# Four modulation vectors gathered as one in the set of step 16, the rows' scales on GpSimd, and a copy of sums moved behind the logarithms

## The chip, the cores and the metric

The kernel runs on one core of one Trainium2 chip. A core has five engines that work side by side, each on its own queue in order: PE (TensorE, matrix products), ACT (ScalarE, activation functions and copies), DVE (VectorE, element by element), POOL (GpSimd, element by element, without access to PSUM) and SP (SyncE, which here only starts DMA transfers). They wait for one another on semaphores. SBUF holds operands, PSUM holds the sums that PE writes. The metric is the time of one execution on the device in microseconds (us), the median of several runs; lower is better.

## What is computed

The reference, cut to what matters here:

```python
mod = (silu(c) @ w_mod).reshape(6, 448)          # six vectors of 448
sa, ca, ga, sb, cb, gb = mod                     # mod[0] ... mod[5] in the kernel
h = layernorm(x) * (1 + ca) + sa                 # x: 2048 tokens x 448 channels
x = x + ga * S4D(h)                              # a long convolution per channel, by FFT in the reference
h = layernorm(x) * (1 + cb) + sb
x = x + gb * mixer(h)                            # token-mixing MLP, 2048 -> 1792 -> 2048
```

`S4D` builds for each of 448 channels a kernel of 2048 taps out of 256 complex exponentials, and convolves. The kernel does the convolution with its own two-stage transform. Since the transform is linear, `ga` is multiplied into the vectors before it: mod[1] becomes (1 + ca) * ga and mod[0] becomes sa * ga.

## The kernel before

The first half of the program makes the convolution kernels, in 56 steps of 8 channels' worth each (`NHALF = 56`). A step `s` needs, of PE, a phase (`st_phase`) and exponents (`st_exponents`), of ACT magnitudes (`st_exp`) and sines (`st_step`), of DVE four products that fill the tile E, of POOL two products that fill the tile G and one (`st_mag2`, tile m), and of PE, two steps later, the sum over both (`st_kgen`, tile kg in PSUM, one buffer). Every second sum is copied by ACT out of PSUM into the tile ks, and POOL adds the skip term every fourth time. E has three buffers in the pool `gp_`, taken in turn.

Exponential and sine are in different function tables of ACT, and loading a table takes time. So the magnitudes of eight steps are made together: `window(s)` at s = 0, 8, 16, 24 and 32 runs the set of eight. It begins with `angle()` and `logs()`, an arctangent and logarithms of the next channels' parameters, then takes `e` from 0 to 7: two magnitudes on ACT (`st_exp`), the next exponents on PE, whatever copies wait in the lists `dve` and `act` (`flush`), some steps of the parameters' chain (`more`, DVE and POOL), and one piece of other work. After the set the steps s to s + 7 follow.

Other work in the sets of steps 8 and 16:

- **Rows** (`u_rows`, 32 of them, L588 on PE and L592 on DVE): the first transform of the layer-normed input. A row takes a table `wur` made on POOL (`u_table`, L571) from the inverse deviation `rs`, and DVE multiplies PE's output by mod[1] and stores it to DRAM (`yu_d`). `rs` is worked out in `logs(True)` by an exponential of a logarithm, and improved by a Newton step in `u_scale`, six small operations on DVE (L552 to L558). `u_means` transforms the means.
- **Columns** (`u_cols`, L624 on PE, L628 on DVE), from step 17 on: the second transform, which reads the rows back and adds mod[0].
- **Modulation** (`modulation(k, half)`): half 0 multiplies the four row blocks of `w_mod` for vector k, each with 32 columns of the activated c, into four blocks of 32 partitions of one PSUM tile (L534, 8 matmul instructions, as each product in this type is two passes), and ACT copies it to SBUF (`parts`, L536). Half 1 adds the four blocks up and spreads them to all partitions by a product with the matrix `sums`, whose rows 0, 32, 64 and 96 are one and the others zero (L530, 2 instructions), and ACT copies this to `mod[k]` (L531). Vectors 1 and 2 are made in steps 4 to 7, vector 0 in the set of step 8, vectors 4, 5 and 3 in the set of step 16.

All these PE outputs (rows, columns, modulation, `st_s1`) take turns in the pool `pms` of three PSUM tiles.

The order on PE, ACT, DVE and POOL is written out by hand (`tc.manual_schedule`): instructions run in the order in which the program emits them. SP is so up to step 8 (`first.close()`); behind it a planner places the DMA starts by its own estimates. `late` gives loads by step: of `w_mod`, vector 2 in step 4, vector 0 in step 7 into a part of the tile `wm0`, vectors 4, 5 and 3 in steps 12 to 14 into parts of `xt` whose rows are done. PE's fillers `warm(n)` (L676) write into the unused half of kg's tile.

At step 7, the sums of step 5 wait to be copied by ACT (L775) and are flushed at the end of the step, in front of the set of step 8:

```python
            if s == NHALF - 1:
                break
            flush(act)
```

and in the set of step 16 the modulation stands at these places:

```python
                for k, e0 in ((4, 1), (5, 3), (3, 6)) if s == 16 else ():
                    if e in (e0, e0 + 1):
                        modulation(k, e - e0)
```

Behind the 56 steps come the rest of the convolution and the token-mixing MLP, which is a long run of matmuls with the weights streamed in.

Of the kernel before, what the change touches and what calls it, by code (L numbers as in the profile page):

```python
# [22 lines left out]
P = 128  # L23
# [209 lines left out]
def tile_adaln_s4d_mixer(ctx, tc, i, out):  # L233
# [19 lines left out]
    with ExitStack() as es:  # L253
# [96 lines left out]
        def wm_slot(k):  # L350
# [8 lines left out]
                wm_load(0, wm_slot(0)),  # L359
# [10 lines left out]
            14: lambda: wm_load(3, xt[0:PP, 8:12, 0:D]),  # L370
        }
# [122 lines left out]
        def logs(root=False):  # L494

            for a, s, u, xa, ya in tmp.values():
                S.activation(u, ya, AF.Square)
                S.activation(s, s, AF.Ln)
                S.activation(u, u, AF.Ln, bias=1.0)
            if root:  # L500
                S.activation(rs, mv[:, :, 1], AF.Ln, bias=eps_t)
                S.activation(rs, rs, AF.Exp, scale=-0.5)
            for q, (a, s, u, xa, ya) in tmp.items():
                S.activation(a, a, AF.Exp, bias=ldt[:, q : q + 1])
            tmp.clear()
# [32 lines left out]

        mv = xp.tile([P, 16, 2], F32, name="mv")
        rs = xp.tile([P, 16], F32, name="rs")  # L540
        nm = xp.tile([P, 16], F32, name="nm")
# [7 lines left out]

        def u_scale():  # L550

            tt(nm, rs, rs, ALU.mult)  # L552
            stt(nm, mv[:, :, 1], EPS, nm, ALU.add, ALU.mult)
            ts(nm, nm, -0.5, 1.5, ALU.mult, ALU.add)
            tt(rs, rs, nm, ALU.mult)
            for h in range(2):
                p = slice(64 * h, 64 * h + 64)
                stt(means[p, h], mv[p, :, 0], -1.0, rs[p], ALU.mult, ALU.mult)  # L558
# [187 lines left out]
        fresh, ready, hold, soon, due = [], [], [], [], []  # L746
# [342 lines left out]
        def window(s):  # L1089
# [3 lines left out]
            logs(s == 8)  # L1093
            if s == 8:
                more(10)
                u_scale()
                u_table(0)
                u_table(1)

            if s == 0:  # L1100
                st_exponents(s)
            for e in range(BATCH):
# [9 lines left out]
                if s == 8 and e == 0:  # L1112
                    tt(mod[1], mod[1], mod[2], ALU.mult)
# [4 lines left out]
                if s == 8 and e in (3, 4):  # L1118
                    modulation(0, e - 3)
                if s == 8 and e == 5:  # L1120

                    G.tensor_tensor(mod[0], mod[0], mod[2], ALU.mult)
# [7 lines left out]
                for k, e0 in ((4, 1), (5, 3), (3, 6)) if s == 16 else ():  # L1130
                    if e in (e0, e0 + 1):
                        modulation(k, e - e0)
# [5 lines left out]
                if s in (8, 16):  # L1138
                    some(u_rows, rows, ((0, 2, 2, 2, 2, 0, 2, 2) if s == 8 else (2, 2, 2, 2, 2, 0, 1, 1))[e])
# [23 lines left out]
        for s in range(NHALF):  # L1163
# [55 lines left out]
            if s == NHALF - 1:  # L1219
                break  # L1220
            flush(act)
# [372 lines left out]
```

## Time and profile before

| what | us |
| --- | --- |
| median of 3 runs (lowest, highest) | 666.34 (666.05, 667.45) |
| the profiled execution, its own time | 666.04 |
| its span in the trace | 664.3 |
| PE busy | 612.2 (92%) |
| DVE busy | 444.1 (67%) |
| ACT busy | 440.9 (66%) |
| POOL busy | 269.5 (41%) |

The span is the time from the first to the last recorded instruction; the rest of the time lies around it. Busy shares over the whole span say little here, since the first half (the steps, up to about 330 us) and the second (the MLP) have different limits: POOL works in the first half only. The views are read by stage: the chain of waits follows the work that ended last back from the end, the timeline lists an engine's instructions (start, length, engine, line, operation, output and inputs, shapes, count, and in brackets the idle time in front and who ended it), and the stretches give each engine's busy time between two times. Lines such as L588 are those of the printed code.

### The profile page before, as it was taken

The page shows a single profiled execution, that of the slowest core. Times are in us where ns is not written, and L with a number is a line of the kernel's source. Part 1 is how long each engine was busy: PE and PEld are TensorE (multiplying, and loading weights), DVE is VectorE, ACT ScalarE, POOL GpSimd, SP SyncE. Part 2 cuts the span into 40 slices and gives each one's busy share as a digit, 9 for nine tenths or more (in the row PEclk, how much of TensorE's full clock was granted, in tenths as well). Part 3 has the DMA queues.
Part 4 walks back from the last instruction along what each step waited for, and adds up shares of the span by engine and source line. Part 5 has one row for each costly group of instructions (what it writes and reads, how often), then busy time and mean ns, then how long its engine had stood idle before and what let it go on. Part 6 is the DMA issues. An engine that isn't in the chain of part 4 may idle for free.

```text
span 664.3 us, 19155 instructions
## 1 busy us (share of the span) xinstructions
PE 612.2 (92%) x7639; PEld 442.8 (67%) x7639; DVE 444.1 (67%) x852; ACT 440.9 (66%) x828; POOL 269.5 (41%) x350
## 2 busy tenths in 40 slices
PE   1868998999999999999898999999999999999997
PEld 0544455445455555656554667788999999999997
DVE  8999889798893877868665677787522553333331
ACT  6978898999889999999587578886222532222220
POOL 7885597498599788797562000000000000000000
PEclk9999999999999999999999989999999999999999
DMA  6695747598876457676787999946665165555530
GB/s 159 195 222 171 271 136 245 213 269 238 230 263 190 66 160 204 186 210 193 236 279 218 257 241 232 218 117 195 181 179 149 59 197 165 162 160 163 166 113 28
DMA packets 98833, 125.14 MB, mean 188 GB/s; under 512 B 13780, under 2 KB 80120, under 8 KB 98744
## 3 DMA queue, kind: packets, MB, share of 16 engines
q1 hardware_dynamic: 97928, 121.30, 64.6%
q0 software_dynamic: 816, 2.62, 1.6%
q8 instruction: 60, 0.98, 0.7%
q14 instruction: 29, 0.24, 0.1%
HBM read 88.53 MB, written 34.87 MB: 186 GB/s over the span
## 4 chain that ended last, share of the span: by engine, by line
PE 58%; ACT 11%; DMA 10%; DVE 7%; POOL 6%; issue 4%; SPq 2%; DVEq 0%; ACTq 0%; POOLq 0%
PE o L1560 7%; PE o L1562 7%; PE o L1561 7%; PE acc L1397 6%; PE acc L1398 6%; PE acc L1399 6%; PE xe L664 5%; PE kg L761 4%; DMA us_d<-uo 3%; PE xg L664 2%; POOL G L734 2%; DMA w<-in_B_w_dram 2%; POOL G L735 2%; PE vv L892 2%; ACT mag L693 2%
## 5 line engine op out<-in xcount | busy, mean ns | idle before, releaser
L218 ACT CAST whi<-w 128x896 fp32r<-128x896 f32 x64 | 59.7, 939 | 138.6 <-PE o L1561 81.5
L227 DVE TENSOR_TENSOR wlo<-w,whi 128x896 fp32r<-128x896 f32 x64 | 68.1, 1086 | 41.8 <-ACT whi L218 38.7
L734 POOL TENSOR_TENSOR G<-mag,gs 128x512 f32<-128x512 f32 x56 | 71.9, 1284 | 37.4 <-ACT gs L730 37.4
L1397 PE MATMUL acc<-h3h,whi 128*128 128x448 f32 x224 | 83.7, 374 | 3.0 <-ACT h3h L1470 1.4
L1398 PE MATMUL acc<-h3l,whi 128*128 128x448 f32 x224 | 81.9, 365 | 0.4 <-DVE mean L1418 0.2
L1399 PE MATMUL acc<-h3h,wlo 128*128 128x448 f32 x224 | 81.6, 364 | 0.0
L1560 PE MATMUL o<-uh,whi 128*128 128x448 f32 x224 | 81.3, 363 | 0.0
L1562 PE MATMUL o<-uh,wlo 128*128 128x448 f32 x224 | 81.2, 362 | 0.0
L1561 PE MATMUL o<-ul,whi 128*128 128x448 f32 x224 | 80.6, 360 | 0.0
L761 PEld LDWEIGHTS kg<-E,G 128*32 128x32 f32 x3584 | 54.2, 111 | 32.9 <-issue 20.9
L735 POOL TENSOR_TENSOR G<-mag,gs 128x512 f32<-128x512 f32 x56 | 72.0, 1287 | 0.0
L761 PE MATMUL kg<-E,G 128*32 128x64 f32 x3584 | 63.5, 222 | 7.5 <-issue 5.4
L664 PE MATMUL xg<-tab,lph 64*128 64x512 f32 x112 | 62.2, 555 | 7.0 <-DVE E L740 3.0
L1565 DVE TENSOR_TENSOR y<-o,x 128x448 f32<-128x448 f32 x16 | 10.0, 625 | 78.8 <-PE o L1562 78.8
L664 PE MATMUL xe<-tab,lph 64*128 64x512 f32 x112 | 62.2, 555 | 0.4 <-issue 0.4
L714 POOL TENSOR_TENSOR m<-mag,w 128x512 f32<-128x512 f32 x53 | 55.8, 1052 | 4.2
L1397 PEld LDWEIGHTS acc<-h3h,whi 128*128 128x128 f32 x224 | 42.5, 190 | 16.2 <-ACT h L1469 3.5
L1398 PEld LDWEIGHTS acc<-h3l,whi 128*128 128x128 f32 x224 | 42.4, 189 | 3.4 <-DVE h3l L1467 0.5
L1399 PEld LDWEIGHTS acc<-h3h,wlo 128*128 128x128 f32 x224 | 42.4, 189 | 3.3
L1562 PEld LDWEIGHTS o<-uh,wlo 128*128 128x128 f32 x224 | 42.1, 188 | 3.4
L1561 PEld LDWEIGHTS o<-ul,whi 128*128 128x128 f32 x224 | 41.9, 187 | 3.0
L1560 PEld LDWEIGHTS o<-uh,whi 128*128 128x128 f32 x224 | 42.0, 188 | 2.1
(256 smaller groups left out, 1391.5 us busy)
## 6 DMA issues: line engine op xcount, KB each, us to landing
w<-in_B_w_dram SPq DMA_DIRECT2D x64, 224.0 KB
w<-in_B_w_dram SPq DMA_DIRECT2D x32, 448.0 KB
yi<-yu_d SPq DMA_DIRECT2D x32, 224.0 KB
us_d<-uo SPq DMA_DIRECT2D x16, 448.0 KB
u<-us_d SPq DMA_DIRECT2D x64, 112.0 KB
v_d<-vt SPq DMA_DIRECT2D x32, 224.0 KB
vt<-v_d SPq DMA_DIRECT2D x14, 448.0 KB
yu_d<-yt SPq DMA_DIRECT2D x13, 448.0 KB
```

Source lines behind the costliest of these rows:

```text
L218: self.nc.scalar.copy(hi, w)
L227: eng.tensor_tensor(lo, w, hi.bitcast(F32), ALU.subtract)
L664: T.matmul(out[k], lhs[r], rhs[r], start=start, stop=stop)
L734: G.tensor_tensor(Gt[:, 1], mg_, v32(sg), ALU.mult)
L735: G.tensor_tensor(Gt[:, 0], mg_, v32(cg_), ALU.mult)
L761: T.matmul(kg[32 * q : 32 * q + 32, m], Gt[:, c, d], E[:, c, d], start=h == 0 and c == 0 and m == 0, stop=h == 1 and c == 1, skip_group_ch ...
L1397: nc.tensor.matmul(acc[f], hi[:, fs], h3h[:, r], start=r == 0, stop=False)
L1398: nc.tensor.matmul(acc[f], hi[:, fs], h3l[:, r], start=False, stop=False)
L1399: nc.tensor.matmul(acc[f], lo[:, fs], h3h[:, r], start=False, stop=r == 15)
L1560: nc.tensor.matmul(o, hi[:, ks], uh[kh][:, k], start=kh == 0 and k == 0, stop=False)
L1561: nc.tensor.matmul(o, hi[:, ks], ul[kh][:, k], start=False, stop=False)
L1562: nc.tensor.matmul(o, lo[:, ks], uh[kh][:, k], start=False, stop=kh == 1 and k == 6)
```

## The change

It has four parts.

1. The four vectors 0, 4, 5 and 3 are made together in the set of step 16. `gathered` adds the four row blocks of each vector up within PSUM, vector n in partitions 32n to 32n + 31 of one tile, in two calls (e = 2, 3) with 16 matmul products in all and one copy to SBUF. `spread` takes the 32 rows of each vector with the same 32 rows of `sums` to all partitions, two vectors per call (e = 4, 6), each with its copy to `mod[k]`. Vector 0's modulation leaves the set of step 8, and its product with mod[2] on POOL moves to e = 6 of the set of step 16. The load of its weights leaves step 7 and goes, in step 16, into a tile of E's ring.
2. The operations of `u_scale` go from DVE to POOL, with two new preparations (`u_ready`: variance plus epsilon, and the negative mean) at the end of step 7. They and the first two row tables are now emitted ahead of ten steps of the parameters' chain. The product mod[1] * mod[2] goes from DVE to POOL.
3. ACT's copy of the sums of step 5 goes from the end of step 7 to between the logarithms and the exponentials in the set of step 8.
4. The rows of the set of step 16 are placed differently: 2, 2, 2, 0, 1, 1, 2, 2 instead of 2, 2, 2, 2, 2, 0, 1, 1 by e, as far as rows are left.

```diff
@@ -356,7 +356,6 @@
         late = {
             4: lambda: wm_load(2, wm_slot(2)),
             7: lambda: [
-                wm_load(0, wm_slot(0)),
                 nc.sync.dma_start(svt, i["SV"]),
                 s2_load(0),
                 s2_load(1),
@@ -368,6 +367,11 @@
             12: lambda: wm_load(4, xt[0:PP, 0:4, 0:D]),
             13: lambda: wm_load(5, xt[0:PP, 4:8, 0:D]),
             14: lambda: wm_load(3, xt[0:PP, 8:12, 0:D]),
+            16: lambda: wm_load(
+                0,
+                gp_.tile([P, 2, GD, NJ], F32, tag="E", name="wE").rearrange("p a g j -> p (a g j)")[0:PP, 0 : 4 * D]
+                .rearrange("p (q d) -> p q d", q=4),
+            ),
         }
 
 
@@ -491,7 +495,7 @@
 
             if q > 1:
                 yield from angles()
-        def logs(root=False):
+        def logs(root=False, inside=()):
 
             for a, s, u, xa, ya in tmp.values():
                 S.activation(u, ya, AF.Square)
@@ -499,6 +503,9 @@
                 S.activation(u, u, AF.Ln, bias=1.0)
             if root:
                 S.activation(rs, mv[:, :, 1], AF.Ln, bias=eps_t)
+            for f in inside:
+                f()
+            if root:
                 S.activation(rs, rs, AF.Exp, scale=-0.5)
             for q, (a, s, u, xa, ya) in tmp.items():
                 S.activation(a, a, AF.Exp, bias=ldt[:, q : q + 1])
@@ -536,9 +543,32 @@
             act.append(lambda: S.copy(pmods[k], pm))
 
 
+        group = (0, 4, 5, 3)
+
+        def gathered(q0):
+
+            if q0 == 0:
+                pmods["all"] = pms.tile([P, D], F32, tag="ms", name="pm")
+            pm = pmods["all"]
+            for q in range(q0, q0 + 2):
+                for n, k in enumerate(group):
+                    T.matmul(pm[32 * n : 32 * n + 32], scb[:, q], wms[k][:, q], start=q == 0, stop=q == 3)
+            if q0:
+                pmods["all"] = qp.tile([P, D], F32, tag="parts", name="parts")
+                act.append(lambda: S.copy(pmods["all"], pm))
+
+        def spread(n0):
+
+            for n in range(n0, n0 + 2):
+                k, r = group[n], slice(32 * n, 32 * n + 32)
+                pm = pms.tile([P, D], F32, tag="ms", name="pm")
+                T.matmul(pm, sums[r], pmods["all"][r], start=True, stop=True)
+                act.append(partial(S.activation, mod[k], pm, AF.Copy, bias=1.0 if k in (1, 4) else 0.0))
+
+
         mv = xp.tile([P, 16, 2], F32, name="mv")
         rs = xp.tile([P, 16], F32, name="rs")
-        nm = xp.tile([P, 16], F32, name="nm")
+        nm, ve, minus = (xp.tile([P, 16], F32, name=k) for k in ("nm", "ve", "minus"))
         means = xp.tile([P, 2, 16], F32, name="means")
         G.memset(means, 0.0)
 
@@ -547,15 +577,20 @@
             V.bn_stats(st, xt[:, r])
             V.bn_aggr(mv[:, r], st)
 
+        def u_ready():
+
+            G.tensor_scalar(ve, mv[:, :, 1], EPS, None, ALU.add)
+            G.tensor_scalar(minus, mv[:, :, 0], -1.0, None, ALU.mult)
+
         def u_scale():
 
-            tt(nm, rs, rs, ALU.mult)
-            stt(nm, mv[:, :, 1], EPS, nm, ALU.add, ALU.mult)
-            ts(nm, nm, -0.5, 1.5, ALU.mult, ALU.add)
-            tt(rs, rs, nm, ALU.mult)
+            G.tensor_tensor(nm, rs, rs, ALU.mult)
+            G.tensor_tensor(nm, ve, nm, ALU.mult)
+            G.tensor_scalar(nm, nm, -0.5, 1.5, ALU.mult, ALU.add)
+            G.tensor_tensor(rs, rs, nm, ALU.mult)
             for h in range(2):
                 p = slice(64 * h, 64 * h + 64)
-                stt(means[p, h], mv[p, :, 0], -1.0, rs[p], ALU.mult, ALU.mult)
+                G.tensor_tensor(means[p, h], minus[p], rs[p], ALU.mult)
 
         def u_means():
 
@@ -743,7 +778,7 @@
 
         kgs, kss, made_k = {}, {}, [0]
 
-        fresh, ready, hold, soon, due = [], [], [], [], []
+        fresh, ready, hold, soon, due, kept = [], [], [], [], [], []
 
         def mellow():
             ready.extend(fresh)
@@ -1090,12 +1125,13 @@
             if s:
                 aside.append(True)
             angle()
-            logs(s == 8)
+            logs(s == 8, kept)
+            kept.clear()
             if s == 8:
-                more(10)
                 u_scale()
                 u_table(0)
                 u_table(1)
+                more(10)
 
             if s == 0:
                 st_exponents(s)
@@ -1110,16 +1146,11 @@
                 flush(dve)
                 flush(act)
                 if s == 8 and e == 0:
-                    tt(mod[1], mod[1], mod[2], ALU.mult)
+                    G.tensor_tensor(mod[1], mod[1], mod[2], ALU.mult)
                 if s < 32:
                     more(WPACE[s // 8][e])
                 if s == 0 and e >= 4:
                     u_stats(e - 4)
-                if s == 8 and e in (3, 4):
-                    modulation(0, e - 3)
-                if s == 8 and e == 5:
-
-                    G.tensor_tensor(mod[0], mod[0], mod[2], ALU.mult)
                 if s and e < (2 if s <= 32 else 1):
                     st_kgen(s - (2 if s <= 32 else 1) + e)
                 elif e == 5 and s < 24:
@@ -1127,16 +1158,20 @@
                         yks[0] = y0.tile([P, 32, DC], F32, tag="yk", name="yk0")
                     st_s1(act)
 
-                for k, e0 in ((4, 1), (5, 3), (3, 6)) if s == 16 else ():
-                    if e in (e0, e0 + 1):
-                        modulation(k, e - e0)
+                if s == 16 and e in (2, 3):
+                    some(u_rows, rows, (2, 0)[e - 2])
+                    gathered(2 * e - 4)
+                elif s == 16 and e in (4, 6):
+                    spread(e - 4)
+                if s == 16 and e == 6:
+                    G.tensor_tensor(mod[0], mod[0], mod[2], ALU.mult)
 
                 if s == 8 and e == 0:
                     warm(7)
                 if s == 8 and e == 1:
                     u_means()
                 if s in (8, 16):
-                    some(u_rows, rows, ((0, 2, 2, 2, 2, 0, 2, 2) if s == 8 else (2, 2, 2, 2, 2, 0, 1, 1))[e])
+                    some(u_rows, rows, ((0, 2, 2, 2, 2, 0, 2, 2) if s == 8 else (2, 2, 0, 0, 1, 1, 2, 2))[e])
                 elif s == 24 and e in (0, 2, 4, 6, 7):
                     some(u_cols, cols, 1)
 
@@ -1218,6 +1253,9 @@
                     piece(False, True)
             if s == NHALF - 1:
                 break
+            if s == 7:
+                kept.append(act.pop())
+                u_ready()
             flush(act)
 
             if s in (1, 2):
```

## The prediction

> **What bounds the kernel now.** I read the page's first lines, then the chain of waits, then the busy time by stretches around the two stages that the diff touches, then the timelines of single engines there.
>
> ```profile
> span 664.3 us, 19155 instructions
> ```
>
> The profiled execution took 666.04 us, 1.74 more than its span. The median of the three runs is 666.34, so a shift of the span by x is forecast as 666.34 + x. The edits lie in the eight-step sets at steps 8 and 16: there all steps' exponents are computed by TensorE and turned into magnitudes on ScalarE, and row and modulation work lies between. First the chain around the set of step 8 (start, length, what):
>
> ```profile
> 66.12 0.99 DVE mod L1113
> ...
> 68.67 1.82 PE pu L588 x4
> ...
> 70.72 0.89 PE pm L534 x8
> 71.61 0.95 PE pu L588 x3
> ...
> 72.95 0.95 PE pm L530 x2
> 73.90 0.96 PE pu L588 x3
> ...
> 82.75 1.28 POOL G L734
> ```
>
> TensorE carries this stage, and both halves of a modulation vector, L534 and L530, are links of it. At 82.75 GpSimd takes over: its work per step sets the pace of the steps behind, so an earlier 82.75 moves all of steps 8 to 15. Now the set of step 16 (per stretch: length, then busy time and count of PE, PEld, DVE, ACT, POOL, then clock, DMA):
>
> ```profile
> 115.00:120.00 5.00, 5.00 (x148) 2.96 (x139) 3.20 (x6) 4.62 (x10) 3.57 (x6) 1.00 0.23 79
> 120.00:125.00 5.00, 4.73 (x22) 1.42 (x18) 4.66 (x11) 4.07 (x8) 3.37 (x8) 1.00 0.84 314
> 125.00:130.00 5.00, 4.84 (x87) 2.46 (x87) 2.81 (x7) 4.88 (x13) 1.59 (x3) 1.00 0.62 228
> ```
>
> PE is busy 14.57 of 15 us, ACT 13.57. Work added to PE there has no cover, and ACT is nearly full itself. The set ends where ACT reaches the first step's work, and GpSimd starts from there:
>
> ```profile
> 133.06 1.27 POOL L734 TENSOR_TENSOR G<-mag,gs 128x512 f32<-128x512 f32 x1 [4.13 <-ACT gs L730]
> ...
> 135.52 0.24 POOL L709 TENSOR_TENSOR w<-mag 128x16 f32<-128x16 f32 x1
> 135.84 1.05 POOL L714 TENSOR_TENSOR m<-mag,w 128x512 f32<-128x512 f32 x1
> 136.84 1.28 POOL L734 TENSOR_TENSOR G<-mag,gs 128x512 f32<-128x512 f32 x1
> ```
>
> GpSimd idles 4.13 us for ACT, then runs back to back, 3.78 us per step. Whatever the set of step 16 loses ahead of 133.06, the rest keeps.
>
> **Part 1: the front of the set of step 8.** ACT and GpSimd as they are:
>
> ```profile
> 59.15 0.37 ACT L775 COPY ks<-kg 128x256 f32<-128x256 f32 x1 [0.83 <-PE kg L676]
> ...
> 63.69 0.21 ACT L502 ACTIVATE rs<-rs 128x16 f32<-128x16 f32 x1
> 65.45 1.18 POOL L571 TENSOR_TENSOR wur<-wu,rs 128x256 f32<-128x256 f32 x2
> 68.73 1.28 DVE L592 SCALAR_TENSOR_TENSOR yt<-pu,means,mod 128x448 f32<-128x448 f32 x2
> ```
>
> The copy of the sums keeps ACT idle 0.83 us for TensorE's filler matmuls. Behind the logarithms it finds them done: the logarithms and the square root's exponential come about 0.84 us earlier (63.69 to 62.85), and so do the first magnitudes and TensorE's next exponents. The copy then ends near 61.6; queued behind it are the exponentials (counted), and on PE the next kernel sums, which need its PSUM tile:
>
> ```profile
> 61.68 1.10 PE L761 MATMUL kg<-E,G 128*32 128x64 f32 x64
> ```
>
> They start at 61.68, so this wait costs nothing to 0.2; I take nothing. Against it, the rows' scales go to GpSimd, ahead of two tables, a split (cast and difference) and now the product that every row's output on DVE needs (formerly DVE's 0.99 at 66.12):
>
> ```profile
> L709 POOL TENSOR_TENSOR w<-mag 128x16 f32<-128x16 f32 x56 | 14.2, 254 | 2.2 <-ACT mag L693 1.3 <-DVE yk L805 0.8
> L401 POOL CAST hl<-xa 128x256 fp32r<-128x256 f32 x2 | 0.8, 398 | 5.8 <-DVE xa L442 5.8
> L403 POOL TENSOR_TENSOR hl<-xa,hl 128x256 fp32r<-128x256 f32 x2 | 1.5, 740 | 0.2
> L1122 POOL TENSOR_TENSOR mod<-mod,mod 128x448 f32<-128x448 f32 x1 | 1.1, 1139 | 1.1 <-ACT mod L531 1.1
> ```
>
> From 63.06: four dependent small operations at 0.32 (135.52 to 135.84 above), two at 0.2, tables 1.18, split 0.40 + 0.74, product 1.14: 63.06 + 1.28 + 0.4 + 1.18 + 1.14 + 1.14 = 68.2, with gaps 68.35. The first row output starts then, not at 68.73: **0.35 gained**. No row shows GpSimd's scalar form, used by one of the six and, in step 7, by the two preparations; I price it as L709, between nothing and the cast's 0.40. The preparations run where GpSimd waits for ACT. Bounds of this part: 0.85 if the product isn't awaited, -0.2 if GpSimd is slower.
>
> [...]
>
> **Part 2: the modulation vector taken out of the set of step 8.** Gone from PE are L534 (0.89 on the chain) and L530 (0.95), with two copies on ACT and a product on GpSimd. Next late would be the ring of three PSUM tiles between PE (1.34 for a pair of rows and its exponents, 71.61 to 72.95) and DVE's outputs (1.28 a pair). The two alternate, so I let 0.2 of the 1.84 come back: **1.65 gained**, bounds 1.2 and 1.84. DVE has 2.0 us less time in this set, and is rid of the product's 0.99 and of six small scale operations; I take it to fit, and a lateness up to 1.2 would be hidden in its wait at step 10:
>
> ```profile
> 89.37 0.69 DVE L736 TENSOR_TENSOR E<-m,xe 128x512 f32<-128x512 f32 x1 [1.24 <-POOL w L709]
> ```
>
> Parts 1 and 2: 82.75 comes **2.0 earlier**, bounds 1.0 and 2.7. The vector's load leaves the queue in step 7, where no step waits for it.
>
> **Part 3: the set of step 16.** PE and ACT now:
>
> ```profile
> 118.28 0.94 PE L534 MATMUL pm<-xt,scb 112*32 112x448 f32 x8
> 119.15 1.02 PE L588 MATMUL pu<-xt,wur 64*128 64x448 f32 x4
> ...
> 120.33 1.02 PE L530 MATMUL pm<-parts,sums 128*128 128x448 f32 x2
> 121.28 0.64 PE L588 MATMUL pu<-xt,wur 64*128 64x448 f32 x1
> 121.29 0.49 PE L664 MATMUL xe<-tab,lex 64*128 64x512 f32 x1
> 121.76 0.54 PE L588 MATMUL pu<-xt,wur 64*128 64x448 f32 x1
> ```
> ```profile
> 123.54 0.53 ACT L536 COPY parts<-pm 128x448 f32<-128x448 f32 x1
> 123.97 0.60 ACT L693 ACTIVATE mag<-xe 128x512 f32<-128x512 f32 x1
> ...
> 126.72 1.07 ACT L805 COPY yk<-y 128x512 f32<-128x512 f32 x2
> 127.68 0.61 ACT L693 ACTIVATE mag<-xe 128x512 f32<-128x512 f32 x1
> ...
> 128.65 0.56 ACT L536 COPY parts<-pm 128x448 f32<-128x448 f32 x1
> 129.06 0.35 ACT L448 ACTIVATE xa<-A_C_real 128x128 f32<-128x128 f32 x1
> ...
> 129.47 0.63 ACT L726 ACTIVATE ab<-xe 128x512 f32<-128x512 f32 x1
> ```
>
> Eight L534 (four row blocks, two passes, column groups side by side) take 0.94. The gather needs 32, so 2 x 1.9, where three vectors took 3 x 0.94. A spread of two vectors takes 1.02 if its quarters run side by side, as the halves do (four L588 in 1.02, where one row's two passes alone take 121.28 to 122.30). Ahead of the first step's phase, PE then has 3.8 + 2.04 against 2.82 + 2.04 (the third old sum came behind it): about 1.0 more.
>
> In the clock of before: the first old gather is gone at 118.28, so a pair of rows starts there; with the exponents between them it takes 1.2 (119.15 to 120.33), the last row 1.0 to 1.15 more, to 120.65. The first gather ends at 122.55, exponents take 0.45 (L664, 0.49 with its fill), and the second gather ends at **124.85**. From here ACT carries it in program order, with the pitches of its rows (0.43 from a copy to the next magnitude, 0.48 from one magnitude to the next): sums' copy 124.95; magnitudes 125.40 to 126.38; two vector copies 126.6 (behind the spread of 125.55 to 126.57) to 127.5; magnitudes to 128.48; two copies of 0.48 to 129.44; magnitudes to 130.4; two vector copies to 131.3; two absolute values; L726 at **131.7** instead of 129.47. That is **2.2 lost**. A copy left out behind L726 doesn't help, since GpSimd paces from its first product. Bounds: 1.0 (the added PE work alone) and 3.2 (quarters one behind the other: 0.55 at ACT in the first spread, some 1.0 in all).
>
> [...] No run here shows 32-row tiles with full width. [...]
>
> The load for the first vector now goes into a tile that the sums of step 13 give back:
>
> ```profile
> 109.90 1.10 PE L761 MATMUL kg<-E,G 128*32 128x64 f32 x64
> ```
> ```profile
> DMA to landing us min/median/max: 3.5/5.4/10.9
> ```
>
> The second row covers all loads of the tile family with the other three vectors. Issued at 111.0, it lands at 116.4 by the median and 121.9 by the longest; the gather wants it at 120.65. Cost nothing, at most 1.25. Queued behind it on SP are the rows' stores and the loads of later exponents; DMA is at a share of 0.23 then, and I price them at nothing, with 0.5 as the upper end if the planner issues it in front of a wait.
>
> **Sum**: -2.0 + 2.2 = **+0.2**, 666.5 us against the median. By the profiled execution: 666.2.
>
> **Rivals.**
> 1. The moved copy doesn't bring its 0.84: GpSimd's product for the rows takes the place of ACT as the last wait entirely. For it: DVE's 68.73 stands only 0.4 behind my 68.35. Gain 1.65 alone, net +0.55: 666.9. Chance 0.14.
> 2. Slower: the late load. The gather stalls in PE with its first matmul, and exponents, magnitudes and GpSimd's start wait behind it, one for one from a landing at 120.65 on. Over 0.2% it needs a landing after 121.8. For it: the 10.9 and the planner's freedom on SP. Against: median 5.4. At a landing of 122.1 the net is +1.65: 668.0. Chance 0.20.
> 3. The quarters run in series: 3.2 lost, net +1.2: 667.5. Chance 0.10, half of it beyond 0.2%.
> 4. Faster: the set of step 16 pays only the added PE work of 1.0, because the sums' copy finds its place in ACT's gaps, and the set of step 8 gains its upper end of 2.7. Net 1.0 - 2.7 = -1.7: 664.6. Against: program order puts the sums' copy ahead of the magnitudes. Chance 0.20.
>
> **How the numbers follow.** The forecast has 0.36. Within 0.2% (1.3 us, about what a measurement of this kernel can tell from no change): 0.36 + 0.14 + 0.05 = 0.55. Slower: 0.20 + 0.05 = 0.25. Faster: 0.20. The terms' bounds give 666.34 + (1.0 - 2.7) = 664.6 up to 666.34 + (3.2 - 1.0) = 668.5, which takes in the late load's 668.0. The median stands 0.3 over the lowest run, and I widen both ends by 0.4: 664.2 to 668.9. The forecast's own range is 665.5 to 667.5.
>
> **What would show it.** Right: GpSimd's first product of step 8 near 80.75; the first row output within 0.1 us of the product on GpSimd that feeds it; steps 8 to 15 as long as before; from the first kernel sums of the set of step 16 (114.8) to GpSimd's first product of step 16 some 2.2 us longer, with ACT idle for the second gather and then full. Wrong: gathers of over 2 us (column groups or load), two spread matmuls starting one after the other, or a pace behind 133.06 that isn't GpSimd's.

## The result, and the profile after

| | median us | lowest to highest | runs |
| --- | --- | --- | --- |
| before | 666.41 | 664.91 to 669.35 | 10 |
| changed | 670.89 | 668.72 to 675.05 | 10 |

The changed kernel takes 1.0073 times as long, with a 95% interval of 1.0050 to 1.0096: slower by about 4.5 us, where 666.5 was forecast. Its profiled run is the longest of the ten, 675.05 us. A second profile of the same kernel (the run e1_again below) is the shortest of its twelve, 667.68. What the two share I put down to the change, and where they differ, to the run.

```profile
span 673.2 us, 19172 instructions
```

The stages, cut at GpSimd's first product (G) of steps 7, 8, 15, 16 and 23. Each row is a stretch: its ends, its length, then busy time and count of PE, PEld, DVE, ACT and POOL, TensorE's mean granted clock, DMA share and GB/s. The kernel before:

```profile
56.93:82.75 25.82, 21.95 (x282) 12.27 (x282) 23.11 (x48) 21.74 (x43) 14.21 (x21) 1.00 0.80 261
82.75:110.21 27.46, 26.28 (x501) 14.91 (x503) 24.01 (x41) 23.40 (x47) 26.77 (x30) 1.00 0.61 191
110.21:133.06 22.85, 21.32 (x402) 11.38 (x392) 18.11 (x38) 21.35 (x42) 11.06 (x18) 1.00 0.59 209
133.06:158.55 25.49, 24.09 (x496) 12.76 (x495) 23.99 (x41) 23.44 (x47) 25.02 (x28) 1.00 0.97 260
```

The changed kernel:

```profile
57.84:82.69 24.85, 21.11 (x272) 12.66 (x271) 18.96 (x40) 20.52 (x41) 16.07 (x30) 0.93 0.61 197
82.69:113.76 31.07, 28.99 (x496) 16.32 (x498) 24.51 (x41) 23.32 (x47) 26.72 (x30) 0.89 0.68 220
113.76:138.32 24.56, 23.07 (x422) 12.45 (x410) 17.64 (x38) 21.20 (x42) 12.06 (x18) 1.00 0.63 211
138.32:164.48 26.16, 23.61 (x480) 12.05 (x480) 22.90 (x39) 22.23 (x45) 25.06 (x28) 0.87 0.92 251
```

The second rows are the surprise. Steps 8 to 15 hold the same work in both kernels and take 3.61 us longer. Their clock is 0.89: (1 - 0.89) x 31.07 = 3.4 us of TensorE's time are missing. Before, all four stretches ran at 1.00. Where the clock went in the changed kernel, in consecutive windows of 3.41 us, the length of the shortest half-clock stretch in its trace (71.61 to 75.03; same columns):

```profile
98.90:102.32 3.42, 3.42 (x78) 1.91 (x76) 3.42 (x7) 3.27 (x7) 3.34 (x5) 1.00 0.99 301
102.32:105.73 3.41, 1.37 (x8) 0.40 (x4) 1.01 (x3) 2.70 (x6) 3.41 (x4) 1.00 0.79 306
105.73:109.14 3.41, 3.39 (x62) 2.10 (x66) 3.41 (x6) 0.61 (x2) 3.33 (x5) 0.50 0.59 183
109.14:112.56 3.42, 3.42 (x27) 1.89 (x17) 1.92 (x4) 0.96 (x2) 0.74 (x2) 0.50 0.92 287
```

In the second window TensorE is busy for 1.37 us only; in the next two the clock is exactly 0.50. What idled it, from the timelines of DVE and PE (start, length, line, operation, count, and in brackets the wait and its releaser):

```profile
105.02 1.28 DVE L627 SCALAR_TENSOR_TENSOR yt<-pu,means,mod 128x448 f32<-128x448 f32 x2 [2.40 <-DMA yu_d<-yt]
```
```profile
105.75 1.86 PE L623 MATMUL pu<-xt,wur 64*128 64x448 f32 x2 [2.06 <-DVE yt L627]
```

VectorE waits 2.40 us for a store to give back a row buffer, and TensorE 2.06 for VectorE. The kernel before has the same two waits at this place, shorter, and full clock behind them:

```profile
104.05 1.28 DVE L592 SCALAR_TENSOR_TENSOR yt<-pu,means,mod 128x448 f32<-128x448 f32 x2 [1.49 <-DMA yu_d<-yt]
```
```profile
104.79 1.02 PE L588 MATMUL pu<-xt,wur 64*128 64x448 f32 x2 [1.16 <-DVE yt L592]
```

At the end of the set of step 8 stands another such chain; the chain of waits of the changed kernel:

```profile
75.49 0.52 issue
76.02 0.58 DVE s L458
...
77.29 1.76 DVE xa L464
...
79.71 0.60 DVE yE L627
80.31 0.04 issue
80.35 1.02 PE pu L623 x2
```

VectorE's parameter operations, with a reciprocal of 1.76 us, stand between the row outputs, and TensorE waits for a free PSUM tile, 0.82 us in this profile. They stood there before too, with a wait of 0.70, but the chain before runs past them, from TensorE's exponents to ScalarE.

### The profile page after: what moved, and what is told of

The parts are those of the page before. It is cut to its first block, busy times and chain, and to the rows that moved or that the text cites. A ratio compares the mean times of both kernels' runs of the same rounds, so it can differ in the third digit from the quotient of the medians.

```text
span 673.2 us, 19172 instructions
## 1 busy us (share of the span) xinstructions
PE 615.9 (91%) x7639; PEld 445.6 (66%) x7639; DVE 441.2 (66%) x845; ACT 438.8 (65%) x825; POOL 272.4 (40%) x359
## 3 DMA queue, kind: packets, MB, share of 16 engines
q0 software_dynamic: 816, 2.62, 1.6%
## 4 chain that ended last, share of the span: by engine, by line
PE 63%; DMA 14%; ACT 6%; DVE 6%; issue 4%; POOL 3%; SPq 3%; ACTq 0%; DVEq 0%; POOLq 0%
PE o L1598 7%; PE o L1600 7%; PE o L1599 7%; PE xe L699 6%; PE acc L1435 6%; PE acc L1436 6%; PE acc L1437 6%; PE kg L796 5%; DMA w<-in_B_w_dram 3%; PE xg L699 3%; PE vv L927 2%; PE pu L623 2%; PE kx L904 2%; DMA us_d<-uo 2%; DMA pars<-hl 2%
## 5 line engine op out<-in xcount | busy, mean ns | idle before, releaser
L796 PEld LDWEIGHTS kg<-E,G 128*32 128x32 f32 x3584 | 56.5, 114 | 38.6 <-issue 26.5
L796 PE MATMUL kg<-E,G 128*32 128x64 f32 x3584 | 66.8, 227 | 11.0 <-issue 7.2
L699 PE MATMUL xg<-tab,lph 64*128 64x512 f32 x112 | 63.6, 568 | 7.7 <-DVE E L775 3.4
L761 ACT ACTIVATE ab<-xe 128x512 f32<-128x512 f32 x56 | 33.9, 605 | 20.2 <-PE xg L699 15.8
L771 DVE TENSOR_TENSOR E<-m,xe 128x512 f32<-128x512 f32 x53 | 36.3, 685 | 15.5 <-issue 4.0
```

Of the source, the lines that this page charges most:

```text
L699: T.matmul(out[k], lhs[r], rhs[r], start=start, stop=stop)
L796: T.matmul(kg[32 * q : 32 * q + 32, m], Gt[:, c, d], E[:, c, d], start=h == 0 and c == 0 and m == 0, stop=h == 1 and c == 1, skip_group_ch ...
```

## The experiments

Two theories stood first. A: the time is lost in stretches of half clock that begin where TensorE waits. B: the work and the waits alone lose it. The kernel before was run beside all of them, with medians of 665.9 to 666.7. Ratios are to that kernel, with 95% intervals.

**The changed kernel again (e1_again)**, no edit.

> The changed kernel once more, for a second profile and more times. Theory A (the granted clock): the work of the two sets costs little; the loss is in stretches at half clock that PE's new waits bring on, and their places vary from run to run. Then the time is 669 to 672 us again, a profile with fewer half-clock stretches between 60 and 150 us than the first one (which had 17 us) is shorter by about half of what they lack, and outside of them the stages are as long as in the first profile. Theory B (work alone): stages as long as in the first profile whatever the clock, and the set of step 16 alone explains over 3 us.

Measured: 671.79 us, 1.0074 [1.0043, 1.0106]. Its profile has the same fault at the other place. TensorE, then the windows:

```profile
79.60 1.02 PE L623 MATMUL pu<-xt,wur 64*128 64x448 f32 x2 [1.87 <-DVE yE L627]
80.55 2.31 PE L711 MATMUL kg<-ones 128*128 128x256 bf16 x10
```
```profile
77.07:80.49 3.42, 1.55 (x7) 0.35 (x3) 3.39 (x7) 3.10 (x5) 0.00 (x0) 1.00 0.87 233
80.49:83.90 3.41, 3.41 (x18) 1.86 (x18) 3.41 (x6) 1.36 (x3) 2.90 (x4) 0.50 0.99 320
```

The kernel before at the same place:

```profile
80.31 1.02 PE L588 MATMUL pu<-xt,wur 64*128 64x448 f32 x2 [0.70 <-DVE yE L592]
81.26 1.26 PE L676 MATMUL kg<-ones 128*128 128x256 bf16 x10
```

A wait of 1.87 instead of 0.70, a window with 1.55 us busy, and half clock in the next: the same ten fillers take 2.31 us instead of 1.26. GpSimd's first products of steps 8 and 9, in e1_again and before:

```profile
80.92 1.27 POOL L769 TENSOR_TENSOR G<-mag,gs 128x512 f32<-128x512 f32 x1 [4.91 <-ACT gs L765]
86.74 1.29 POOL L769 TENSOR_TENSOR G<-mag,gs 128x512 f32<-128x512 f32 x1 [1.99 <-ACT gs L765]
```

```profile
82.75 1.28 POOL L734 TENSOR_TENSOR G<-mag,gs 128x512 f32<-128x512 f32 x1 [6.48 <-ACT gs L730]
86.55 1.28 POOL L734 TENSOR_TENSOR G<-mag,gs 128x512 f32<-128x512 f32 x1
```

They are 5.82 us apart, against 3.80. Step 8 starts 1.8 us earlier than before, and step 15 at 110.09 against 110.21: the gain is gone. At step 13, where the first profile lost its time, VectorE has no wait for a store here.

**One part at a time (e2_four, e3_front).** e2_four keeps the change's parts 1 and 4 (the four vectors, the rows' places) and undoes 2 and 3; e3_front does the reverse.

```diff
 # e2_four, against the changed kernel
-            if s == 7:
-                kept.append(act.pop())
-                u_ready()
...
-                    G.tensor_tensor(mod[1], mod[1], mod[2], ALU.mult)
+                    tt(mod[1], mod[1], mod[2], ALU.mult)
```

> The kernel before with the four vectors gathered in the set of step 16 (and its load and rows), but without the move of the scales to GpSimd and of the copy. Theory A: the set of step 8 gains 1.6 us as computed; if the half-clock stretches come with the set of step 16 and the steps behind it, 668 to 670 us, if they come with GpSimd's late product, 665.5 to 667. Theory B: 1.65 gained and 2.2 lost, 667 us.

> The kernel before with only the scales and the product on GpSimd and the copy behind the logarithms. Theory A: PE waits over 1 us for the product on GpSimd and is granted half clock behind it; 667.5 to 669 us. Theory B: 0.35 gained at most and no more than 0.9 lost: 666 to 667.3 us.

Measured: e2_four 668.93, 1.0047 [1.0014, 1.0081]; e3_front 665.32, 0.9991 [0.9957, 1.0025]. Alone, the front part makes no difference that can be measured (its median lies below both forecasts), and the four vectors lose. Whether both together lose more than the vectors alone can't be told from these intervals. In e2_four VectorE's wait for the store is 2.77 us, a half-clock stretch runs from 105.0 to 108.4, and steps 8 to 15 take 30.30 us.

**Fillers (e4_fill)**: eight more early in the set of step 8, ten more at steps 16 and 17.

```diff
+                if s == 8 and e == 2:
+                    warm(8)
...
-                    warm(10)
+                    warm(20 if s in (16, 17) else 10)
```

> The changed kernel with more filler matmuls where PE waits: 8 ahead of the second pair of rows in the set of step 8, 10 more each at steps 16 and 17 (their output is used by nothing). Theory A: the half-clock stretches near 75 and 140 us go, and 1.5 to 3 us against the changed kernel with them: 668 to 669.5 us. Theory B: no gain, or up to 1 us lost to the fillers: 671 to 672 us.

Measured: 671.17, 1.0071 [1.0038, 1.0104]. The eight ran some 9 us ahead of the wait at the end of the set; the half-clock stretch (81.4 to 84.8) came as before, behind a wait of 1.88. This told nothing against A, only that the place was wrong.

**VectorE's chain earlier (e5_chain).**

```diff
-        WPACE = [[0, 2, 2, 1, 1, 1, 1, 1], [2, 2, 2, 2, 1, 3, 3, 1], [4] * 7 + [9], [4] * 8]
+        WPACE = [[0, 2, 2, 1, 1, 1, 1, 1], [4, 4, 1, 4, 3, 0, 0, 0], [4] * 7 + [9], [4] * 8]
```

> The changed kernel, with VectorE's parameter chain of the set of step 8 shared out over the columns as 4, 4, 1, 4, 3, 0, 0, 0 in place of 2, 2, 2, 2, 1, 3, 3, 1: nothing of it is then queued ahead of the last row outputs of that set. Theory C (the set of step 8 is 2.2 us shorter as forecast, and the steps 8 to 15 give it back through two waits of VectorE, the chain at the end of the set and the store at step 13, each of which also draws a half-clock stretch): the idle time of TensorE at the last rows of the set, 1.87 us in the second run of the changed kernel, falls under 0.9; from GpSimd's first product of step 8 to that of step 9 it takes 3.8 to 4.4 us and not 5.8; the time falls by 0.7 to 1.8 us, to 669.5 to 670.8. Rival D (the half-clock stretches come at any wait, so that the next one takes the place of this one): the first distance is short, but that from step 8 to step 15 stays at 29 to 31 us, and the time at 671 to 672.

Measured: 674.79, 1.0105 [1.0059, 1.0152], a clear miss. The chain now stood ahead of more row outputs, and TensorE waited longer:

```profile
81.51 1.11 PE L623 MATMUL pu<-xt,wur 64*128 64x448 f32 x1 [4.74 <-DVE yE L627]
```

Half clock from 81.4 to 88.2 followed; the set of step 8 took 31.19 us. Steps 8 to 15, at full clock behind it, took 27.16.

**Vector 5's load later (e6_store, e7_both, e8_best)**, alone, with the edit of e5_chain, and with both on the front part.

```diff
-            13: lambda: wm_load(5, xt[0:PP, 4:8, 0:D]),
...
+            15: lambda: wm_load(5, xt[0:PP, 12:16, 0:D]),
```

> The changed kernel, with the load of vector 5's weights put into the room of the last four row groups, which comes free two steps later: the row stores of steps 12 and 13 then stand ahead of it in SyncE's queue. Theory C: VectorE's wait for the store at step 13 (2.40 us in the profiled run of the changed kernel) falls under 1 us; from step 14 to step 15 GpSimd takes 2.9 to 3.5 us and not 6.5; the distance from step 8 to step 15 falls by 1 to 2 us on the mean; the time falls by 0.5 to 1.8 us, to 669.5 to 671.0. If the later load were late for the gathers of the set of step 16, the distance from step 15 to step 16 would grow over 24.6 us. Rival D: the stall goes, another wait draws the stretch, and the time stays at 671 to 672.

> Both edits of the two runs before, in the changed kernel. Theory C: from step 8 to step 15 it takes 27.0 to 28.2 us, as in the kernel before (27.46), and not 29 to 31; what is left is the gain of 2.2 in the set of step 8 and the loss of 1.2 to 1.7 in that of step 16: the time is 666.5 to 668.5, within 0.3% of the kernel before. Rival D: 670 to 672.

> The front part alone (the copy behind the logarithms, the scales and the product on GpSimd; the four vectors stay one per gather as in the kernel before) with the same two edits. Theory C: the set of step 8 is about 0.2 to 0.5 us shorter than before, the waits of VectorE go, and nothing is lost in the set of step 16: 663.5 to 665.3, ratio 0.995 to 0.999. Rival D: 665 to 667, no difference to the kernel before that can be measured.

Measured: 673.55, 1.0096 [1.0061, 1.0130]; 676.56, 1.0164 [1.0119, 1.0209]; 671.74, 1.0082 [1.0044, 1.0119]. In these three the load stands in program order ahead of the rows that read the same room, so the last rows work on the weights in place of the tokens, and wait for them. From e6_store:

```profile
120.14 1.12 PE L623 MATMUL pu<-xt,wur 64*128 64x448 f32 x2 [3.19 <-DMA xt<-in_w_mod_dram]
```

Their totals say nothing of the store; only their stages ahead of that wait are used below.

**The waits taken away cleanly (e9_chain_late, e10_load_act, e11_both, e12_front_both)**: the seven last parameter operations go behind the set, or vector 5's load goes to ScalarE's queue at step 15, into its old room, or both, in the changed kernel and in the front part.

```diff
-        WPACE = [[0, 2, 2, 1, 1, 1, 1, 1], [2, 2, 2, 2, 1, 3, 3, 1], [4] * 7 + [9], [4] * 8]
+        WPACE = [[0, 2, 2, 1, 1, 1, 1, 1], [2, 2, 2, 2, 1, 0, 0, 0], [4] * 7 + [9], [4] * 8]
```
```diff
-            13: lambda: wm_load(5, xt[0:PP, 4:8, 0:D]),
...
+            15: lambda: wm_load(5, xt[0:PP, 4:8, 0:D], nc.scalar),
```

> The changed kernel, with the seven parameter operations of VectorE that stand among the last row outputs of the set of step 8 (sum to floor, 4.3 us with the reciprocal's 1.75) put two by two behind the products of steps 8 to 11. Theory C (they hold the last row outputs back, TensorE waits for a free bank, and the wait draws a half-clock stretch): TensorE's idle time at the last rows of the set falls from 1.87 us to under 0.7, no half-clock stretch lies between step 8 and step 10, and the first products of GpSimd for step 8 and for step 15 are 28 us apart or less, where four runs with this change had 29.2 to 31.1. The median falls by 1 to 2.5 us, to 668.5 to 670.8 (the changed kernel: 670.9 and 671.8). Rival E (VectorE is itself full in steps 8 to 11, so that the same 4.3 us cost there what they cost before): the two products are 29 to 31 us apart and the median stays over 670.8.

> The changed kernel, with the 784-KB load of vector 5's weights issued two steps later, from ScalarE's queue at step 15 and not from SyncE's at step 13, into the same room. Theory C: the row stores issued at about 96 and 99 us land sooner, VectorE's wait for one of them at step 13 (2.40 us in the profiled run of the changed kernel, 1.49 in the kernel before) falls under 1 us, and no half-clock stretch begins between 100 and 112 us; the median falls by 0.3 to 1.5 us, to 669.5 to 671. Rival F (the store's time is its own and that of its neighbours, not the load's): the wait stays within 0.5 us of 1.5 to 2.4 and the median at 671 to 672.

> The changed kernel with both edits. Theory C: GpSimd's first products of step 8 and step 15 are 27.0 to 28.0 us apart (27.46 before); what is left is the gain of 2.2 us in the set of step 8 and the loss of 1.2 to 1.7 in the set of step 16, so that the median is 665.8 to 668, no more than 0.25% above the kernel before, and may lie under it. Rivals E and F: 669.5 or more.

> The front part alone (copy behind the logarithms, scales and product on GpSimd; every vector with a gather of its own, as in the kernel before) with both edits. Theory C: the waits of VectorE are smaller in this kernel (1.81 us at step 13, no half-clock stretch after it), so the edits bring 0 to 1.5 us: median 663.8 to 665.3 where the front part alone had 665.3 and the kernel before 666.4. Rival E: 665.3 to 667.

Measured: 670.82, 1.0068 [1.0037, 1.0099]; 673.05, 1.0076 [1.0042, 1.0110]; 677.75, 1.0154 [1.0108, 1.0201]; 671.59, 1.0063 [1.0034, 1.0093]. The wait that each edit aimed at is gone from its profile, and none helped. The wait for the store, of 1 us or more, shows in none of the six profiles in which vector 5's load was moved and in nine of the twelve others; e1_again is one of the three without it, so the load is likely to be its cause, but not shown to be. In e9_chain_late the first products of steps 8 and 9 are 4.12 us apart, without half clock there. But the moved operations, with two on ScalarE, now stand among the work of the steps, and TensorE waits there, once for ScalarE and once for VectorE:

```profile
84.62 0.46 PE L699 MATMUL xg<-tab,lph 64*128 64x512 f32 x1 [2.14 <-ACT xg L767]
...
90.04 0.49 PE L699 MATMUL xg<-tab,lph 64*128 64x512 f32 x1 [2.06 <-DVE E L775]
```

Half clock came at 90.6 and again at 107.7, and steps 8 to 15 took 33.44. In e12_front_both, which makes the four vectors as before, the same two waits came (2.13 and 1.85), with half clock behind the second. In e10_load_act the wait for the store was gone and steps 8 to 15 took 27.22 at full clock, but TensorE stopped in the middle of the sums in the set of step 16, with nothing to wait for that the profile shows:

```profile
121.73 1.49 PE L796 MATMUL kg<-E,G 128*32 128x64 f32 x42 [2.73 <-issue]
```

Half clock ran there too (121.5 to 125.0), and that set took 28.13. Theory C of these texts falls as a way to the time: with one wait removed, another wait or a pause came in a later place.

**Fillers in the waits (e13_fill_waits).**

```diff
+                if s == 8 and e == 7:
+                    warm(12)
...
+            if s in (12, 13):
+                warm(10)
```

> The changed kernel with 12 filler matmuls (some 1.5 us) ahead of TensorE's last rows of the set of step 8 and 10 (some 1.3 us) ahead of its rows at steps 12 and 13, where it waits for VectorE. Theory A (the lost time is half-clock stretches that begin where TensorE waits): no half-clock stretch begins between 77 and 110 us, GpSimd's first products of steps 8 and 15 are 27.2 to 28.5 us apart, and the median falls to 667.5 to 669.5. Theory B (the waits themselves lose the time): the distance stays at 29 us or more, or grows by the fillers, and the median is 671 or more.

Measured: 672.57, 1.0075 [1.0047, 1.0103]. The windows around the end of the set:

```profile
75.01:78.42 3.41, 3.41 (x77) 2.19 (x75) 2.96 (x5) 3.17 (x8) 1.25 (x3) 1.00 0.73 274
78.42:81.84 3.42, 3.42 (x25) 1.93 (x23) 2.87 (x7) 3.08 (x5) 0.00 (x0) 1.00 0.78 184
81.84:85.25 3.41, 3.41 (x85) 2.42 (x83) 3.41 (x6) 2.94 (x7) 2.59 (x3) 1.00 1.03 357
```

TensorE is never idle in these windows, the clock stays at 1.00 from 75 to 116 us, and steps 8 to 15 take 28.72 us, 20 more fillers included. So no half clock began where the waits were filled, as A had it, and the edit adds work to TensorE alone. The 28.72 lies between A's 28.5 and B's 29: at full clock 1.26 us more than before were still lost. But the set of step 16 then took 28.22, with a pause of 1.83 and half clock from 116.0 to 122.8, and the median didn't fall. As a forecast of the time, A's expectation missed.

**The pause near 46 us (e14_changed_load, e15_front_load, e16_before_load)**: vector 2's load two places earlier on SP, in three kernels.

```diff
-            4: lambda: wm_load(2, wm_slot(2)),
+            3: lambda: wm_load(2, wm_slot(2)),
```

> The changed kernel with the 784-KB load of vector 2's weights two places earlier in SyncE's queue, ahead of a pair of small loads. In every profile so far TensorE pauses 3 to 4 us near 46 us with nothing to wait for that the trace shows, right behind this load's issue, and the clock is halved for 3.4 to 6.8 us from 47 to 50 us on. Theory G (the pause is TensorE's instruction load queued behind the 784 KB): it falls under 1.5 us, the half-clock stretch behind it goes, and the median falls by 2 to 4 us against the changed kernel, to 667 to 669. If the pause isn't the load's: no difference, 671 to 672.

> The front part alone with the same move of vector 2's load. Theory G: 661.5 to 663.5, faster than the kernel before by 0.4 to 0.7% and faster than the changed kernel. If the pause isn't the load's: 665 to 666.

> The kernel before with the same move and nothing else. Theory G: 662.5 to 664.5, ratio 0.994 to 0.997. If the pause isn't the load's: no difference.

Measured: 672.53, 1.0070 [1.0037, 1.0104]; 667.40, 1.0003 [0.9975, 1.0032]; 666.40, 0.9990 [0.9956, 1.0025]. The pause stayed (4.25, 3.56 and 3.87 us): it isn't the load's. The profiles still serve, as three more draws of where half clock falls. In e14_changed_load the same wait of 1.87 as in e1_again drew no half clock:

```profile
79.85:83.26 3.41, 1.66 (x12) 0.92 (x9) 3.34 (x7) 3.08 (x5) 0.00 (x0) 1.00 0.79 287
83.26:86.68 3.42, 3.30 (x24) 1.73 (x24) 3.42 (x8) 2.36 (x5) 1.97 (x2) 1.00 0.91 204
```

GpSimd's first products of steps 8 and 9 in this profile:

```profile
84.71 1.28 POOL L769 TENSOR_TENSOR G<-mag,gs 128x512 f32<-128x512 f32 x1 [4.91 <-ACT gs L765]
...
88.97 1.28 POOL L769 TENSOR_TENSOR G<-mag,gs 128x512 f32<-128x512 f32 x1 [0.40 <-ACT gs L765]
```

They are 4.26 us apart, where e1_again had 5.82 and the kernel before 3.80. Up to here the two kernels differ only in the place of a load at steps 3 and 4. So with the same wait of TensorE, the half clock cost 1.56 us and the longer wait by itself 0.46.

**All profiles together.** Each cell: length of the stage in us and, in brackets, its mean granted clock, from the same four stretches as above.

| kernel | set of step 8 | steps 8 to 15 | set of step 16 | steps 16 to 23 |
| --- | --- | --- | --- | --- |
| before | 25.82 (1.00) | 27.46 (1.00) | 22.85 (1.00) | 25.49 (1.00) |
| e16_before_load | 26.32 (0.94) | 27.21 (1.00) | 22.68 (1.00) | 25.50 (1.00) |
| e3_front | 25.61 (1.00) | 28.17 (1.00) | 22.85 (1.00) | 25.50 (1.00) |
| e15_front_load | 27.13 (0.94) | 28.97 (0.94) | 22.83 (1.00) | 25.48 (1.00) |
| e12_front_both | 27.13 (0.94) | 30.81 (0.94) | 23.46 (1.00) | 25.41 (0.93) |
| e8_best | 29.98 (0.94) | 27.16 (1.00) | 22.94 (1.00) | 25.50 (1.00) |
| changed | 24.85 (0.93) | 31.07 (0.89) | 24.56 (1.00) | 26.16 (0.87) |
| e1_again | 23.60 (0.99) | 29.17 (0.95) | 24.01 (1.00) | 25.49 (1.00) |
| e2_four | 23.08 (1.00) | 30.30 (0.94) | 24.31 (1.00) | 25.51 (1.00) |
| e4_fill | 23.58 (1.00) | 30.79 (0.94) | 25.65 (1.00) | 25.48 (1.00) |
| e14_changed_load | 23.61 (1.00) | 31.08 (0.95) | 24.25 (1.00) | 25.50 (1.00) |
| e13_fill_waits | 24.87 (0.93) | 28.72 (1.00) | 28.22 (0.88) | 25.48 (0.93) |
| e9_chain_late | 23.39 (1.00) | 33.44 (0.90) | 25.22 (0.93) | 25.47 (0.93) |
| e10_load_act | 24.95 (0.93) | 27.22 (1.00) | 28.13 (0.94) | 25.80 (0.87) |
| e11_both | 25.02 (0.93) | 30.77 (0.94) | 31.88 (0.84) | 25.70 (0.87) |
| e5_chain | 31.19 (0.89) | 27.16 (1.00) | 23.91 (1.00) | 25.48 (0.93) |
| e6_store | 24.00 (0.90) | 30.33 (0.91) | 28.64 (0.88) | 25.51 (1.00) |
| e7_both | 31.59 (0.78) | 27.16 (1.00) | 25.83 (0.93) | 25.50 (1.00) |

Steps 8 to 15 take 27.16 to 28.72 us in the eight profiles with full clock there and 28.97 to 33.44 in the ten without. In the upper six rows, where each vector has its own gather, two have a stretch of half clock in steps 8 to 15 and none in the set of step 16; in the lower twelve there are eight and six, the six all in kernels with a further edit, and two of them (e6_store, e7_both) behind the wait for the weights.

At step 13 the waits alone cost more than at the end of the set. From step 14 to step 15 GpSimd's first products are 2.90 us apart before and 2.62 in e1_again, which has no wait for the store. At full clock with such a wait they are 3.66 (e3_front) and 4.24 (e4_fill) apart; with half clock as well, 4.45 to 6.72 (e15_front_load, e2_four, e14_changed_load, changed, e9_chain_late). Over steps 16 to 23, where GpSimd sets the pace, clocks of 0.87 to 0.93 cost between nothing and 0.7 us.

## Why the prediction was wrong

- **Front of the set of step 8: 0.35 forecast, about nothing found.** The copy did its part: the exponential of the inverse deviation starts 5.80 us behind the first product of step 7 (57.84 to 63.64), where it was 6.76 (56.93 to 63.69). The term that was too small is GpSimd's: its small operations take 2.24 us up to the tables (63.94 to 66.18), where 1.68 was priced. So the product becomes the last wait, as the first rival had it. In the changed kernel's timelines VectorE's first row output starts 0.03 us behind the product on GpSimd:

```profile
68.48 1.13 POOL L1149 TENSOR_TENSOR mod<-mod,mod 128x448 f32<-128x448 f32 x1
```
```profile
69.64 1.27 DVE L627 SCALAR_TENSOR_TENSOR yt<-pu,means,mod 128x448 f32<-128x448 f32 x2 [2.28 <-POOL mod L1149]
```

  That is 11.80 us behind the first product of step 7 (57.84), as before (56.93 to 68.73). e3_front has the set 0.21 shorter.
- **Vector 0 out of the set of step 8: right way, more than forecast.** In e2_four, which has it without the front part, the set takes 23.08 us instead of 25.82: 2.74 gained, above the bound of 1.84. With the front part it is 2.2 (23.58 and 23.61 at full clock). The 2.0 forecast for parts 1 and 2 together so came out nearly right by two misses that cancel. These are single profiles, and why the gain is this large stays open.
- **Set of step 16: 2.2 lost forecast, 1.1 to 1.7 found** (23.91 to 24.56 at full clock without more fillers, against 22.85), inside the bounds. In the changed kernel's TensorE timeline:

```profile
124.19 0.58 PE L555 MATMUL pm<-xt,scb 112*32 112x448 f32 x3
...
127.42 0.55 PE L555 MATMUL pm<-xt,scb 112*32 112x448 f32 x3
128.65 1.02 PE L565 MATMUL pm<-parts,sums 32*128 32x448 f32 x4 [0.25 <-ACT parts L558]
```

  Both gathers, with the exponents between them, take 3.8 us (124.19 to 127.97), where 4.2 was forecast (120.65 to 124.85), and two spreads, 32-row tiles at full width, take 1.02, the quarters side by side, as long as the halves' four L588 in the kernel before. The load of vector 0 is issued at 114.69, and its gather doesn't wait for it. The second and third rivals fell.
- **The step that failed: "steps 8 to 15 as long as before".** With it the whole gain of 2.0 was carried to the end. In the two profiles of the changed kernel these steps took 31.07 and 29.17 us, where 27.46 was expected. The prediction let a lateness of VectorE up to 1.2 us be "hidden in its wait at step 10". It looked at VectorE's own slack, and not at TensorE, which stands behind VectorE through the PSUM tiles and the row buffers. There TensorE waited longer: 1.87 us at the end of the set in e1_again (0.70 before), 2.06 at step 13 in the first profile (1.16 before). Behind each of these two waits the clock was halved for 3.4 us or more, in a stage where TensorE is busy for 26.28 of 27.46 us. No term and no rival spoke of the clock, although the profile of the kernel before gives it.
- **The sum.** At full clock the stages alone give -2.2 + 1.4 = -0.8, where +0.2 was forecast, and within its bounds. Over the runs of all experiments the mean granted clock is 0.985 before (111 runs) and 0.977 and 0.978 changed (10 and 12 runs). That is 5 us more of missing TensorE time per run, as much as three more stretches of 3.41 us at half clock, and the means differ by 4.5 us (671.1 against 666.6). Runs of equal clock show how much goes with it: at 0.979 to 0.982 the kernel before has a mean of 668.5 us (26 runs) and the changed one 670.3 (8 runs). By this estimate 1.8 of the 4.5 us don't go with the clock, and 2.7 do. A missing microsecond doesn't cost the same everywhere: by the table, nearly nothing in steps 16 to 23.

That half clock lengthens steps 8 to 15 is shown by one pair of profiles with the same wait (5.82 and 4.26 us). That the waits lengthen them at full clock too is shown between steps 14 and 15 by e3_front and e4_fill; so theories A and B each hold in part. How the 4.5 us divide is estimated from runs of equal clock and not shown: no kernel kept the clock up in all stages, so none gave the loss back. No version beat the kernel before by more than the measurement resolves.

## What to carry to other kernels

Time saved on the engine that carries a stage is worth something only if the engines that free its buffers are as early; look for who it will wait for next, and for how long. If TensorE is nearly full behind that wait, price the wait and the half-clock stretch that can follow: here, in the two profiles of the changed kernel, with TensorE waiting 1.87 and 2.06 us, the stage took 1.7 and 3.6 us longer than before for both together. Judge such a change by many runs and by the granted clock per stage, since one profile of it may be the best or the worst run.

## What the hardware showed

- In the profiles of before and changed every half-clock stretch between 20 and 335 us is 3.41 or 6.83 us long, and their starts stand on a grid. In the changed kernel they start at 47.72, 71.61, 105.75, 139.88, 228.63 and 290.07 us: the distances are 7.00, 10.00, 10.00, 26.00 and 18.00 times 3.413. Before, they start at 32.26, 49.32 and 213.16, which is 5.00 and 48.00 times. In e1_again the edges 32.7, 36.1, 49.75, 53.2, 80.5 and 83.9 us all leave 1.9 to 2.0 when divided by 3.413, where the starts above leave 3.4 (changed) and 1.5 to 1.6 (before): the grid lay elsewhere in each of these three.
- Waits shorter than 3.41 us came ahead of half clock: 1.87 and 2.06 us in the two profiles of the changed kernel. In the profiles of before and changed nine half-clock stretches begin between 20 and 335 us. In the 3.41 us ahead of eight of them TensorE was busy for 0.61 to 2.09 us; ahead of the ninth (213.16 before) it was busy throughout. At full clock on the same grids, nine stretches of 3.41 us with 2.16 to 2.46 us busy were not followed by half clock, and neither was one with 1.66 in e14_changed_load. So the busy time alone doesn't tell where half clock comes.
- The times of one kernel spread over 7.6 us (667.68 to 675.24 in e1_again), and the longer runs have the lower clock: of the kernel before, 29 runs at 0.982 or less have a mean of 668.8 us, 26 runs at 0.988 or more one of 664.9.
- In the profiles of before, changed and e13_fill_waits to e16_before_load TensorE stops for 3.09 to 4.25 us in the middle of the sums of one step between 44 and 53 us, in each six matmuls before their end, with no releaser in the trace. Pauses of this kind come in other sums too (121.73 above; 1.17 us ahead of 166.67 before, 1.82 ahead of 290.23 in the changed kernel). Moving the load that is issued just ahead changed nothing (3.56 to 4.25). The traces hold a lead: the four such pauses of over 0.9 us between 20 and 340 us in the profiles of before and changed end 1.36 to 1.64 us behind the landing of a 16-KB transfer on a DMA queue that the profile names instruction. Whether TensorE waits for that transfer, no run tested.
- Each of ScalarE's 22 loads of a function table took 1.28 us, before as in the changed kernel; at the front of the set of step 8 the kernel before has two (60.16 and 62.40).
- GpSimd worked on SBUF alone: none of its 350 instructions before and 359 in the changed kernel has a PSUM tile as output or input. What it could do with one, no run shows.
